# Running the first MoE1 chunk in two halves of 256 tokens, with a new order of attention units and other PSUM banks

## The chip, the cores and the metric

The kernel runs on one core of one Trainium2 chip. The metric is the device time of one execution in microseconds (us), lower is better. Times of one kernel spread by up to 2.4 us here, so comparisons below are against runs of the kernel before on the same chip, in the same rounds, unless the text says otherwise. Engine names as in the profile: PE is TensorE, PEld its weight loads, ACT is ScalarE, DVE is VectorE, POOL is GpSimd, SP is SyncE.

## The reference

Sliding-window attention with ALiBi (8 batches, 8 heads, 576 tokens, head size 64, window 128) feeds a two-layer gated MLP over all 4608 tokens:

```python
scores = scale * q @ k.T + slopes[h] * -(pos_q - pos_k)   # only 0 <= pos_q - pos_k < 128
attn   = softmax(scores) @ v
x      = attn, as [4608 tokens, 512]
h      = x @ w_in            # 512 -> 2048, "MoE1" in the kernel
g      = h * cos(h)
out    = g @ w_out           # 2048 -> 512, "MoE2"
```

## The kernel before

The kernel records operations with their data dependencies and a priority. A list scheduler of its own then fixes one static order per engine, and semaphores are put in where engines depend on each other. PE executes its list strictly in that order.

Tokens go through the MLP in nine chunks of 512. Chunk `c` is worked on while attention for batch `c + 1` runs, so most attention work hides beside matmuls. Chunk 0 has no such cover: attention for batch 0 has to be done first. It has nine units: `(pr, G)` is head pair `pr` with queries `256*G` to `256*G + 255`, and `"t"` is the tail, queries 512 to 575, of all heads.

```python
def units(b):
    if b == 0:
        return [(pr, G) for p0 in range(2) for G in range(2) for pr in (p0, p0 + 2)] + [
            ("t", None)]
    return [("t", None)] + [(pr, G) for pr in range(NPAIR) for G in range(2)]
```

Each unit is: scores (PE), exponential (ACT), mask product (DVE), product with v (PE), normalization (DVE), transposition back into `xT` (PE, then a copy by ACT or DVE). MoE1 needs all four pairs, as they are its contraction dimension:

```python
def moe1(c, fc, bank):
    ...
    for kc in range(NPAIR):
        op("pe", lambda e, kc=kc: e.matmul(
            ps[:, bank, :], w_in[:, kc, 128 * fc:128 * fc + 128], xT[:, kc, r0:r0 + CH],
            start=(kc == 0), stop=(kc == NPAIR - 1)), ...)      # 512 columns
    op("act", ... ACTF.Sin, bias=halfpi ...)                    # cos, 128x512
    op("dve", ... gT[gi][:, fc, :] = ps * cos ...)              # 128x512
...
if c == 0:
    for fc in range(NFC):                                       # 16 groups
        moe1(c, fc, (OB + UB)[fc % 4])
    for pl in range(2):
        qk_transposes("q", pl, SB[0:2])
        qk_transposes("k", pl, SB[2:4])
```

There are eight PSUM banks: `SB` (4 to 7) for scores, `UB` (2, 3) for products with v and the transpositions back, `OB` (0, 1) for MoE2 results. In chunk 0 a MoE1 group uses one of banks 0 to 3, and two of these belong to attention until its tail is done. One more rule of the scheduler matters: exponential and cosine are functions of different tables on ACT, and all exponentials of a batch come before the first cosine of the chunk.

The softmax here doesn't subtract the row's maximum and nothing guards it: scores larger than these inputs give would overflow.

Of the kernel before, what the change touches and what calls it, by code (L numbers as in the profile page):

```python
# [6 lines left out]
ALU = mybir.AluOpType  # L7
ACTF = mybir.ActivationFunctionType
# [3 lines left out]
B, H, S, D = 8, 8, 576, 64  # L12
NPAIR = H // 2
# [4 lines left out]
NFC = DFF // 128  # L18
CH = 512
# [15 lines left out]
class Plan:  # L35
# [12 lines left out]
    def op(self, eng, fn, r=(), w=(), dma=None, occ=100, lat=None, pri=5, mode=0, table=None):  # L48
        o = Op()
        o.seq = len(self.all)  # L50
        o.eng = (eng,) if isinstance(eng, str) else tuple(eng)
        o.fn, o.r, o.w, o.dma = fn, tuple(r), tuple(w), dma
        o.occ, o.lat, o.pri, o.mode, o.table = occ, occ if lat is None else lat, pri, mode, table
        preds = {}
        for k in o.r:
            if k in self.writer:
                preds[self.writer[k]] = DATA
        for k in o.w:
            if k in self.writer:
                preds[self.writer[k]] = DATA  # L60
            for d in self.readers.get(k, ()):
                preds.setdefault(d, WAR)
        if dma is not None and dma in self.lastdma:
            preds[self.lastdma[dma]] = DATA
        if eng in ("pool", "sp"):
            if eng in self.lastseq:
                preds.setdefault(self.lastseq[eng], ORDER)
            self.lastseq[eng] = o
        if dma is not None:
            self.lastdma[dma] = o  # L70
        o.preds, o.succs, o.npred = preds, [], len(preds)
        for d in preds:
            d.succs.append(o)
        for k in o.r:
            self.readers.setdefault(k, []).append(o)
        for k in o.w:
            self.writer[k], self.readers[k] = o, []
        self.all.append(o)
        return o
# [160 lines left out]
def bass_alibi_sliding__then__act_gcu_kernel(  # L240
# [8 lines left out]
    with ExitStack() as ctx:  # L249
# [4 lines left out]
        op = R.op  # L254

        w_in = sb("w_inb", [128, 4, DFF])
        w_out = sb("w_outb", [128, NFC, DMODEL])
        XR = 3 * CH
        xT = sb("xT", [128, NPAIR, XR])
        gT = [sb(f"gT{i}", [128, NFC, CH]) for i in range(2)]  # L260
# [11 lines left out]
        NCOS = 3  # L272
        cosb = [sb(f"cos{i}", [128, 512], F32) for i in range(NCOS)]
# [90 lines left out]
        def qk_transposes(which, pl, banks):  # L364
            jj = ((0, 5), (5, 9))

            def dst(n):
                return ps[:, banks[n], :].bitcast(BF16)[:, 0:128 * (jj[n][1] - jj[n][0])]

            def f(e):  # L370
                ins = None
                for n, (j0, j1) in enumerate(jj):
                    for j in range(j0, j1):
                        for x in range(2):
                            ins = e.transpose(  # L375
                                dst(n)[64 * x:64 * x + 64, 128 * (j - j0):128 * (j - j0) + 128],
                                qB[which][:, 2 * pl + x, 64 * j:64 * j + 64], ident[:, :])
                return ins
            op("pe", f, r=[("qB", which, pl), "ident"], w=[("B", x) for x in banks],
               occ=500, lat=670, mode=2, pri=3)  # L380
            for n, (j0, j1) in enumerate(jj):
                o = tr[which][:, :].rearrange("p (g l t) -> p g l t", g=2, l=2)[
                    :, :, pl, 0:576].rearrange("p g (s j) -> p g s j", j=9)[:, :, :, j0:j1]
                i = dst(n).rearrange("p (j g s) -> p g s j", j=j1 - j0, g=2)
                op(("act", "dve"),
                   {"act": lambda e, o=o, i=i: e.activation(o, i, ACTF.Copy),  # L386
                    "dve": lambda e, o=o, i=i: e.tensor_copy(o, i)},
                   w=[("B", banks[n]), ("tr", which, pl, j0)],
                   occ={"act": (730, 620)[n], "dve": (750, 620)[n]},
                   lat={"act": (840, 735)[n], "dve": (815, 690)[n]}, pri=4)  # L390
# [6 lines left out]

        def units(b):
            if b == 0:
                return [(pr, G) for p0 in range(2) for G in range(2) for pr in (p0, p0 + 2)] + [  # L400
                    ("t", None)]
            return [("t", None)] + [(pr, G) for pr in range(NPAIR) for G in range(2)]

        def scores(b, us):
# [140 lines left out]
        def xkeys(pr, t0, n):  # L545
            return [("xT", pr, (t // 64) % (XR // 64)) for t in range(t0, t0 + n, 64)]
# [42 lines left out]
        ccount = [0]  # L589

        def moe1(c, fc, bank):
            ci = ccount[0] % NCOS
            ccount[0] += 1
            gi = c % 2
            r0 = (CH * c) % XR
# [3 lines that stand above are left out]
                    start=(kc == 0), stop=(kc == NPAIR - 1)),  # L599
                   r=xkeys(kc, CH * c, CH) + [("wi", fc // 4)], w=[("B", bank)],  # L600
                   occ=216, lat=379, pri=5)
            op("act", lambda e: e.activation(cosb[ci][:, :], ps[:, bank, :], ACTF.Sin,  # L602
                                             bias=halfpi[:, 0:1]),
               r=["halfpi"], w=[("B", bank), ("cos", ci)], occ=586, lat=687, table=2 * c + 1,
               pri=3)
            op("dve", lambda e: e.tensor_tensor(gT[gi][:, fc, :], ps[:, bank, :], cosb[ci][:, :],  # L606
                                                ALU.mult),
               r=[("cos", ci)], w=[("B", bank), ("g", gi, fc)], occ=606, lat=692, pri=3)

        def moe2(c):  # L610
            gi = c % 2
            for t in range(4):
                tg = 4 * c + t
                bank = OB[tg % 2]
                oi = tg % NOB
                for fc in range(NFC):
                    op("pe", lambda e, t=t, fc=fc, bank=bank: e.matmul(  # L617
                        ps[:, bank, :], gT[gi][:, fc, 128 * t:128 * t + 128], w_out[:, fc, :],
                        start=(fc == 0), stop=(fc == NFC - 1)),
                       r=[("g", gi, fc), ("wo", fc // 4)], w=[("B", bank)], occ=216, lat=379,  # L620
                       pri=6)
                op(("act", "dve"),
                   {"act": lambda e, bank=bank, oi=oi: e.activation(  # L623
                       ob[oi][:, :], ps[:, bank, :], ACTF.Copy),
                    "dve": lambda e, bank=bank, oi=oi: e.tensor_copy(ob[oi][:, :], ps[:, bank, :])},
                   w=[("B", bank), ("ob", oi)], occ={"act": 490, "dve": 606},
                   lat={"act": 591, "dve": 691}, pri=6)
                row = CH * c + 128 * t
                op("sp", [lambda e, oi=oi, row=row: e.dma_start(out[row:row + 128, :],
                                                                ob[oi][:, :])],  # L630
                   r=[("ob", oi)], dma=f"st{oi}", occ=60, lat=600)
# [34 lines left out]
        for c in range(NCH):  # L666
            if c < B - 1:
                if c == 0:
                    for fc in range(NFC):
                        moe1(c, fc, (OB + UB)[fc % 4])  # L670
                    for pl in range(2):
                        qk_transposes("q", pl, SB[0:2])
                        qk_transposes("k", pl, SB[2:4])
                else:
                    qk_transposes("q", 0, SB[0:2])
                    qk_transposes("k", 0, SB[2:4])
                    for fc in range(NFC):
                        if fc == 8:
                            qk_transposes("q", 1, SB[0:2])
                        if fc == 12:  # L680
                            qk_transposes("k", 1, SB[0:2])
                        moe1(c, fc, (UB + SB + UB + SB[2:] + UB + SB[2:] + UB)[fc])
                if c + 2 < B:
                    for pl in range(2):
                        load_qk("q", q, c + 2, pl)
                        load_qk("k", k, c + 2, pl)
                    load_v(c + 2, (3, 4, 0, 1, 2))
                attention(c + 1)
            else:
                for fc in range(NFC):  # L690
                    moe1(c, fc, (UB + SB)[(16 * c + fc) % 6])
            moe2(c)
# [29 lines left out]
```

## Time and profile before

| | before |
|---|---|
| median time | 353.36 us (353.24 to 354.44, 3 runs) |
| span of the profiled run | 351.4 us |
| PE busy | 334.0 us, 95% |
| PE idle from 80 to 340 us | 0.50 us |
| tail exponential of batch 0 ends | 25.46 us |
| first cosine starts | 31.63 us |
| last MoE1 matmul of chunk 0 | 47.4 us |

The page of the profile: the span, the busy times with their shares, then the busy tenths of PE in 40 equal slices and the granted clock in tenths.

```profile
span 351.4 us, 7156 instructions
...
PE 334.0 (95%) x2912; PEld 167.2 (48%) x2912; DVE 206.2 (59%) x451; ACT 236.2 (67%) x347; POOL 79.8 (23%) x121
...
PE   2768999999999999999999999999999999999996
```

PE is full from the fifth slice on. What can be won lies in the first four slices, about 35 us. The table of stretches of PE alone gives them in finer steps; the columns are the stretch in us, its length, PE's busy time with its instruction count, the granted clock, the DMA share and GB/s.

```profile
20.00:22.00 2.00, 2.00 (x18) 1.00 1.24 206
22.00:24.00 2.00, 1.54 (x36) 1.00 1.24 206
24.00:26.00 2.00, 0.98 (x24) 1.00 1.23 206
26.00:28.00 2.00, 1.37 (x13) 0.60 1.22 205
28.00:30.00 2.00, 1.90 (x6) 0.55 1.21 203
30.00:32.00 2.00, 1.53 (x36) 1.00 1.21 203
32.00:60.00 28.00, 27.43 (x272) 1.00 1.42 175
```

PE idles about 2.7 us between 22 and 32 us, and its clock falls to about half at 26 to 30 us. From 32 to 60 us only 0.57 us are idle. The clock column shows 1.00 wherever the trace holds no clock record yet; here the first record is a rise to full at 22.98 us, and PE ran at half speed before it (experiments 1 and 6 come back to this). The timeline of ACT (start, duration, engine and line, operation, out from in, count, and in brackets the idle time before with what ended it):

```profile
24.43 1.03 ACT L447 ACTIVATE ptail<-ps 128x1024 bf16<-128x1024 f32 x1
26.92 0.72 ACT L583 ACTIVATE xT<-ps 128x256 bf16<-128x256 bf16 x2 [1.45 <-PE ps L569]
29.94 0.38 ACT L583 ACTIVATE xT<-ps 128x256 bf16<-128x256 bf16 x1 [2.30 <-PE ps L569]
30.34 1.28 ACT L602 ACT_TABLE_LOAD   x1
31.63 1.27 ACT L602 ACTIVATE cos<-ps,halfpi 128x512 f32<-128x512 f32 x2
```

ACT ends its last exponential at 25.46 us, then waits 1.45 and 2.30 us for PE, because the copies into `xT` stand ahead of the table load in its order. The timeline of PE:

```profile
27.79 1.90 PE L597 MATMUL ps<-xT,w_inb 128*128 128x512 bf16 x4
...
38.13 9.45 PE L597 MATMUL ps<-xT,w_inb 128*128 128x512 bf16 x43
47.42 4.05 PE L617 MATMUL ps<-w_outb,gT 128*128 128x512 bf16 x18
51.89 0.19 PE L491 MATMUL ps<-vp,ptail 128*128 128x65 bf16 x1 [0.42 <-DVE ptail L463]
```

The first line is MoE1 at half clock: 1.90 us for four matmuls, whose modelled ends overlap; in the chain of waits (from the last instruction back, at each step to what released it) they take 1.71 us, 0.43 us each. The 43 matmuls of the second line take 9.40 us in that chain, 0.219 us each. The last line shows the largest later gap before 60 us, 0.42 us.

### The profile page before, as it was taken

What the parts mean: (1) busy time and instruction counts of PE and PEld (TensorE: products, weight loads), DVE (VectorE), ACT (ScalarE), POOL (GpSimd) and SP (SyncE); (2) the same over time, 40 slices, a digit from 0 to 9 for tenths busy, and PEclk for the clock granted to TensorE, in tenths of its full rate; (3) what the DMA queues carried; (4) which work ended last, traced back from release to release, by engine and by line L of the source; (5) the groups of instructions that cost most, each with busy time, mean ns of one, the idle gap of its engine ahead of it and who ended that gap; (6) DMA issues with size and microseconds to landing.
All of it is one profiled execution on the core that took longest, in us unless ns stands there. A gap on an engine that the chain in (4) does not pass through costs nothing.

```text
span 351.4 us, 7156 instructions
## 1 busy us (share of the span) xinstructions
PE 334.0 (95%) x2912; PEld 167.2 (48%) x2912; DVE 206.2 (59%) x451; ACT 236.2 (67%) x347; POOL 79.8 (23%) x121
## 2 busy tenths in 40 slices
PE   2768999999999999999999999999999999999996
PEld 2434445544644554455445644464445444444442
DVE  2486768677858777793576645692768254065000
ACT  3875888987878788877667876786777564155121
POOL 8993700252207021602150207000000000000000
PEclk9998999999999999999999999999999999999999
DMA  6999999449148833915291329400011000100212
GB/s 91 163 207 205 194 186 107 69 68 98 36 93 89 103 48 49 131 47 97 48 137 43 73 55 118 81 32 29 2 41 52 0 32 17 74 32 30 90 62 90
DMA packets 56160, 28.25 MB, mean 80 GB/s; under 512 B 39232, under 2 KB 51520, under 8 KB 56128
## 3 DMA queue, kind: packets, MB, share of 16 engines
q0 software_dynamic: 50944, 18.36, 47.0%
q1 hardware_dynamic: 5184, 9.44, 7.2%
q8 instruction: 23, 0.38, 0.4%
q14 instruction: 9, 0.07, 0.1%
HBM read 36.70 MB, written 9.44 MB: 131 GB/s over the span
## 4 chain that ended last, share of the span: by engine, by line
PE 90%; ACT 3%; DVE 2%; POOL 2%; DMA 1%; issue 1%; POOLq 0%; ACTq 0%
PE ps L597 37%; PE ps L617 33%; PE ps L375 5%; PE ps L425 5%; PE ps L505 3%; PE ps L569 2%; PE ps L508 2%; DMA krows<-in_k_dram 1%; ACT ptail L447 1%; DVE ptail L463 1%; PE ps L491 1%; ACT L447 1%; POOL qrows L298 1%; PE ps L415 1%; PE ps L493 1%
## 5 line engine op out<-in xcount | busy, mean ns | idle before, releaser
L617 PE MATMUL ps<-w_outb,gT 128*128 128x512 bf16 x576 | 138.7, 379 | 0.0
L597 PE MATMUL ps<-xT,w_inb 128*128 128x512 bf16 x576 | 137.7, 382 | 0.0
L606 DVE TENSOR_TENSOR gT<-ps,cos 128x512 bf16<-128x512 f32 x144 | 92.1, 686 | 70.5 <-PE ps L617 55.9
L602 ACT ACTIVATE cos<-ps,halfpi 128x512 f32<-128x512 f32 x144 | 93.2, 689 | 29.0 <-PE ps L617 13.4
L597 PEld LDWEIGHTS ps<-xT,w_inb 128*128 128x128 bf16 x576 | 52.2, 98 | 62.8 <-DVE gT L606 7.3
L617 PEld LDWEIGHTS ps<-w_outb,gT 128*128 128x128 bf16 x576 | 53.9, 98 | 58.7 <-issue 2.2
L455 ACT ACTIVATE p<-ps 128x768 bf16<-128x768 f32 (+1 forms) x64 | 56.2, 916 | 16.4 <-PE ps L425 15.5
L298 POOL DMA_DIRECT2D qrows<-in_q_dram x32 | 19.8, 634 | 129.3 <-PE ps L375 61.6
L623 ACT ACTIVATE ob<-ps 128x512 f32<-128x512 f32 x31 | 18.5, 597 | 44.7 <-PE ps L617 44.7
L470 DVE TENSOR_TENSOR p<-p,emask 128x768 bf16<-128x768 bf16 (+1 forms) x64 | 39.3, 617 | 2.0 <-ACT p L455 1.9
L307 POOL DMA_DIRECT2D vp<-in_v_dram x40 | 34.1, 906 | 0.0
L539 DVE TENSOR_TENSOR xnat<-ps,rec 128x256 bf16<-128x256 f32 x64 | 26.4, 418 | 0.5
L505 PE MATMUL ps<-vp,p 128*128 128x65 bf16 x256 | 22.9, 199 | 0.8 <-DVE xT L584 0.4
L425 PE MATMUL ps<-qt,kt 64*128 64x128 bf16 (+1 forms) x320 | 20.6, 253 | 1.5 <-ACT kt L386 1.0
L505 PEld LDWEIGHTS ps<-vp,p 128*128 128x128 bf16 x256 | 17.0, 100 | 9.8 <-DVE xT L584 3.4
L298 POOL DMA_DIRECT2D krows<-in_k_dram x32 | 19.6, 636 | 8.5 <-PE ps L597 7.5
L569 PE MATMUL ps<-ident,xnat 128*128 128x128 bf16 x128 | 18.5, 229 | 2.7 <-DVE xnat L539 2.7
L583 ACT ACTIVATE xT<-ps 128x256 bf16<-128x256 bf16 (+3 forms) x36 | 12.6, 353 | 12.0 <-PE ps L569 11.8
L508 PE MATMUL ps<-vp,p 128*128 128x65 bf16 x192 | 20.6, 197 | 0.0
L386 ACT ACTIVATE kt<-ps 128x640 bf16<-128x640 bf16 (+1 forms) x21 | 15.8, 777 | 4.3 <-PE ps L375 4.3
L375 PE MATMUL ps<-ident,qrows 128*64 128x128 bf16 x288 | 12.1, 233 | 6.0 <-POOL ident L339 6.0
L537 DVE RECIPROCAL rec<-ps 128x4 f32<-128x4 f32 x64 | 11.2, 178 | 8.7 <-PE ps L508 7.3
(44 smaller groups left out, 200.2 us busy)
## 6 DMA issues: line engine op xcount, KB each, us to landing
out_dram<-ob SPq DMA_DIRECT2D x36, 256.0 KB, 2.0
qrows<-in_q_dram POOLq DMA_DIRECT2D x32, 144.0 KB, 3.4
krows<-in_k_dram POOLq DMA_DIRECT2D x32, 144.0 KB, 4.1
vp<-in_v_dram POOLq DMA_DIRECT2D x32, 128.0 KB, 4.5
w_inb<-in_moe_w_in_dram POOLq DMA_DIRECT2D x4, 512.0 KB, 10.0
w_outb<-in_moe_w_out_dram POOLq DMA_DIRECT2D x4, 512.0 KB, 18.5
vp<-in_v_dram POOLq DMA_DIRECT2D x8, 64.0 KB, 4.2
```

The lines of the kernel that those rows point to most:

```text
L298: fns.append(lambda e, g=g: e.dma_start(qB[which][64 * g:64 * g + 64, 2 * pl:2 * pl + 2, :], src[b, 4 * g + 2 * pl:4 * g + 2 * pl + 2, :, ...
L307: op("pool", [lambda e, t=t, rows=rows: e.dma_start(vp[b % 2][0:rows, t, :, 0:64], v[b, :, 128 * t:128 * t + rows, :].rearrange("h p d -> ...
L375: ins = e.transpose(dst(n)[64 * x:64 * x + 64, 128 * (j - j0):128 * (j - j0) + 128], qB[which][:, 2 * pl + x, 64 * j:64 * j + 64], ident[: ...
L425: ins = e.matmul(ps[:, banks[x], c0:c1], keys_ap(x, pr, kc), query_ap(x, pr, qb, 128 * nb), start=True, stop=True)
L455: op("act", lambda e: e.activation(P[i][:, :, lo:512], src_[:, :, lo:512], ACTF.Exp, scale=0.125), w=held + [("P", i)], occ=920 if u[1] el ...
L470: op("dve", lambda e: e.tensor_tensor(P[i][:, :, lo:512], P[i][:, :, lo:512], EM[:, 2 * pr:2 * pr + 2, lo:512], ALU.mult), r=[("P", i), (" ...
L505: ins = e.matmul(o, P[i][:, x, d0:d0 + 128], V[:, kc, h, 0:65], start=True, stop=not two)
L508: ins = e.matmul(o, P[i][:, x, p0:p0 + 128], V[:, kc - 1, h, 0:65], start=False, stop=True)
L597: op("pe", lambda e, kc=kc: e.matmul(ps[:, bank, :], w_in[:, kc, 128 * fc:128 * fc + 128], xT[:, kc, r0:r0 + CH], start=(kc == 0), stop=(k ...
L602: op("act", lambda e: e.activation(cosb[ci][:, :], ps[:, bank, :], ACTF.Sin, bias=halfpi[:, 0:1]), r=["halfpi"], w=[("B", bank), ("cos", c ...
L606: op("dve", lambda e: e.tensor_tensor(gT[gi][:, fc, :], ps[:, bank, :], cosb[ci][:, :], ALU.mult), r=[("cos", ci)], w=[("B", bank), ("g", ...
L617: op("pe", lambda e, t=t, fc=fc, bank=bank: e.matmul(ps[:, bank, :], gT[gi][:, fc, 128 * t:128 * t + 128], w_out[:, fc, :], start=(fc == 0 ...
```

## The change

Its intent: work for PE should be there earlier. The units of batch 0 are reordered so that the first queries of all pairs come first; MoE1 of chunk 0 runs in two halves of 256 tokens, so that half 0 needs four units instead of eight; and its groups use six banks, the score banks included, once the scores are done. A group now holds two values of `fc` for 256 tokens, so the cosines and products keep shape and count.

```diff
-                return [(pr, G) for p0 in range(2) for G in range(2) for pr in (p0, p0 + 2)] + [
-                    ("t", None)]
+                return [(pr, G) for G in range(2) for pr in (0, 2, 1, 3)] + [("t", None)]
@@ new, beside moe1, used for chunk 0 only (cut)
+        def moe1_half(c, hf, f2, bank):
+            ...
+            t0 = CH * c + 256 * hf
+            for i in range(2):
+                fc = 2 * f2 + i
+                for kc in range(NPAIR):
+                    op("pe", lambda e, i=i, fc=fc, kc=kc: e.matmul(
+                        ps[:, bank, 256 * i:256 * i + 256], w_in[:, kc, 128 * fc:128 * fc + 128],
+                        xT[:, kc, r0:r0 + 256], start=(kc == 0), stop=(kc == NPAIR - 1)),
+                       r=xkeys(kc, t0, 256) + [("wi", fc // 4)], w=[("B", bank)], ...)
+            op("act", ... cosine of 128x512 ...)
+            op("dve", ... product into gT[gi][:, 2 * f2:2 * f2 + 2, 256 * hf:256 * hf + 256] ...)
@@ moe2 waits for its half only
-                       r=[("g", gi, fc), ("wo", fc // 4)], ...
+                       r=[("g", gi, fc, t // 2), ("wo", fc // 4)], ...
@@ chunk 0
-                    for fc in range(NFC):
-                        moe1(c, fc, (OB + UB)[fc % 4])
+                    for i in range(NFC):
+                        moe1_half(c, i // 8, i % 8, (OB + SB)[i] if i < 6 else (OB + SB)[i % 4])
                     for pl in range(2):
-                        qk_transposes("q", pl, SB[0:2])
+                        qk_transposes("q", pl, SB[2:4])
                         qk_transposes("k", pl, SB[2:4])
```

More of the change, by code (lines that the diff above doesn't have):

```diff
@@ L607, in moe1 @@
                                                 ALU.mult),
-               r=[("cos", ci)], w=[("B", bank), ("g", gi, fc)], occ=606, lat=692, pri=3)
+               r=[("cos", ci)], w=[("B", bank), ("g", gi, fc, 0), ("g", gi, fc, 1)], occ=606, lat=692, pri=3)
+        def moe1_half(c, hf, f2, bank):
+            ci = ccount[0] % NCOS
+            ccount[0] += 1
+            gi = c % 2
+            t0 = CH * c + 256 * hf
+            r0 = t0 % XR
+            for i in range(2):
[4 more added lines that the diff above has]
+                        xT[:, kc, r0:r0 + 256], start=(kc == 0), stop=(kc == NPAIR - 1)),
+                       r=xkeys(kc, t0, 256) + [("wi", fc // 4)], w=[("B", bank)],
+                       occ=108, lat=271, pri=5)
+            op("act", lambda e: e.activation(cosb[ci][:, :], ps[:, bank, :], ACTF.Sin,
+                                             bias=halfpi[:, 0:1]),
+               r=["halfpi"], w=[("B", bank), ("cos", ci)], occ=586, lat=687, table=2 * c + 1,
+               pri=3)
+            op("dve", lambda e: e.tensor_tensor(
+                gT[gi][:, 2 * f2:2 * f2 + 2, 256 * hf:256 * hf + 256],
+                ps[:, bank, :].rearrange("p (i t) -> p i t", i=2),
+                cosb[ci][:, :].rearrange("p (i t) -> p i t", i=2), ALU.mult),
+               r=[("cos", ci)], w=[("B", bank)] + [("g", gi, 2 * f2 + i, hf) for i in range(2)],
+               occ=606, lat=692, pri=3)
         def moe2(c):
@@ L619, in moe2 @@
                         start=(fc == 0), stop=(fc == NFC - 1)),
-                       r=[("g", gi, fc), ("wo", fc // 4)], w=[("B", bank)], occ=216, lat=379,
+                       r=[("g", gi, fc, t // 2), ("wo", fc // 4)], w=[("B", bank)], occ=216, lat=379,
                        pri=6)
```

## The prediction

> **What bounds the kernel now.** TensorE. The page's busy table gives PE 334.0 us of a 351.4 us span (95%), and the busy table by stretches shows PE idle for only 0.5 us of the 240 us between 80 and 320 us. So the time is "when PE becomes dense" plus a fixed amount of PE work. The lost time is at the start: the timeline shows PE gaps until about 30.5 us (PE busy 2.68 of 5 us at 15-20, 3.92 at 20-25, 3.86 at 25-30), and the granted clock falls to 0.60 and 0.55 at 26-30 us, where a 512-column matmul takes 0.43 us instead of 0.216. One later gap, 0.42 us at 51.5 us, waits for the mask of the next batch's tail.
>
> Why PE starves: MoE1 of chunk 0 needs all 512 tokens, that is all eight attention units; the last xT copies end at 30.3 us. Only 8 of its 64 matmuls are done by 32.3 us, its first cosine runs at 31.6 us (the table load waits behind those copies, 30.3-31.6), and its last matmul ends at 47.4 us.
>
> **What the change does.** First-query units of all four head pairs go first, so half 0 of MoE1 can start when four units are done. 64 matmuls of 512 columns become 128 of 256: the same columns, so about 0.108 us each (half of 0.216, an estimate); 64 more weight loads (98 ns each) stay under the matmuls, as the page shows PEld at 48%. The Trainium skill, "TensorE: Matmul & The Clock Gate", section on throughput, gives N/2.4 + 2.5 ns for an isolated gap, so at most 0.2 us extra in all. Cosines (0.69 us) and products (0.69 us) keep their count, 16. Six PSUM banks can hold half 0, so PE may run six groups before a cosine ends. Two q transposes move banks; negligible.
>
> **Size.** ACT still has to do the mask exponentials, eight unit exponentials and the tail; I expect its tail exponential to end at 25-25.5 us as before (25.46). But the table load now follows at once, so cosines start near 26.8 instead of 31.6 us. W_in quarters landed at 19.9, 22.1, 24.7 and 27.4 us (issue plus landing time), just soon enough. PE then has dense work from about 26.4 us: 112 half matmuls 12.1 us, q/k transposes 4 x 0.62, remaining attention 1.2 us, about 0.5 us stalls on ACT/DVE (16 cosines plus five q/k copies fill ACT for about 14 us in the same stretch). MoE1 ends at about 42.6 us. Before, it ended at 47.4, 0.5 us of that being next-batch scores that now come later: gain about 4.3 us. The 0.42 us gap should vanish, as 23 instead of 18 MoE2 matmuls cover that chain. W_out (last quarter 43.4 us) and the next v (44.2-48.0 us) should land just before use. All saved time is PE-critical, nothing later gives it back.
>
> **Prediction:** 348.9 us, 80% range 346.7 to 351.2. Faster by over 2% 0.08, within 2% 0.91, slower by over 2% 0.01.
>
> **What would show the steps right:** MoE1 matmuls of 128x256 spaced about 0.108 us once the clock is up; first cosine at 26-28 us; granted clock near 1.0 in 25-30 us; last MoE1 matmul at 41.5-44 us; no PE gap before the next tail's product; PE busy total about unchanged or slightly lower while the span falls by 4-5 us; from 60 us on the same stream, shifted.
>
> **What would make it wrong:** PE, in order, stuck behind a MoE1 matmul waiting for w_in while scores wait behind it, delaying the exponentials; the clock staying at half until 30 us (costs up to 2 us); ACT and DVE, nearly full at 26-42 us, pacing the MoE1 groups; DMA (about 205 GB/s up to 40 us) bringing w_out or v too late; 256-column matmuls slower than half.

(The section of the Trainium skill meant there, in "TensorE: Matmul & The Clock Gate", is "Back-to-back issue gap". The 0.2 us is an estimate from that page's 2.5 ns: 64 more matmuls make 0.16 us.)

## The result

| | before | changed |
|---|---|---|
| median time, same rounds | 353.81 us (4 runs) | 349.19 us (348.81 to 349.53, 4 runs) |
| ratio, first comparison | | 0.9869 (95%: 0.9845 to 0.9892) |
| ratio, repeated in other rounds (below) | | 0.9864 (0.9845 to 0.9883) |
| span of the profiled run | 351.4 us | 346.8 us |
| PE busy | 334.0 us | 331.8 us |
| tail exponential of batch 0 ends | 25.46 us | 25.56 us |
| first cosine starts | 31.63 us | 26.87 us |
| last MoE1 matmul of chunk 0 | 47.4 us | 42.6 us |

A ratio is the mean time of one kernel's fast runs over that of the other's of the same rounds, so it is not quite the ratio of the medians quoted. At 1.3% the change is within the 2% that count as the same, but clear of noise.

The page of the changed kernel:

```profile
span 346.8 us, 7278 instructions
...
PE 331.8 (96%) x2976; PEld 172.4 (50%) x2976; DVE 203.9 (59%) x452; ACT 235.7 (68%) x346; POOL 79.6 (23%) x121
...
PE   2689999999999999999999999999999999999996
```

PE is full one slice earlier. Its table of stretches:

```profile
20.00:22.00 2.00, 2.00 (x19) 1.00 1.25 207
22.00:24.00 2.00, 1.72 (x31) 1.00 1.24 206
24.00:26.00 2.00, 2.00 (x43) 1.00 1.23 205
26.00:28.00 2.00, 2.00 (x27) 1.00 1.22 204
28.00:30.00 2.00, 1.85 (x29) 1.00 1.23 210
30.00:32.00 2.00, 2.00 (x25) 1.00 1.19 199
32.00:60.00 28.00, 28.00 (x372) 1.00 1.41 176
```

The hole is gone, and the clock no longer falls. From 32 to 60 us PE has no idle time at all, so neither w_out nor v came late. The timeline of ACT:

```profile
24.53 1.03 ACT L446 ACTIVATE ptail<-ps 128x1024 bf16<-128x1024 f32 x1
25.58 1.28 ACT L624 ACT_TABLE_LOAD   x1
26.87 1.27 ACT L624 ACTIVATE cos<-ps,halfpi 128x512 f32<-128x512 f32 x2
```

The table load follows the last exponential at once. The timeline of PE:

```profile
30.05 2.67 PE L619 MATMUL ps<-xT,w_inb 128*128 128x256 bf16 x23
...
40.16 2.58 PE L619 MATMUL ps<-xT,w_inb 128*128 128x256 bf16 x22
42.57 1.89 PE L642 MATMUL ps<-w_outb,gT 128*128 128x512 bf16 x8
```

The last line is the first of MoE2: MoE1 ends there. The MoE1 matmuls of 256 columns cost just half of those of 512: 2.51 us for 23 in the chain of waits is 0.109 us each. The Trainium skill ("TensorE: Matmul & The Clock Gate", section "Back-to-back issue gap") gives N/2.4 + 2.5 ns for an isolated gap at full clock, an estimate of 109.2 ns for 256 columns; the trace agrees.

The chain of waits of the changed kernel (start, duration, what), from the stretch before PE becomes dense:

```profile
20.49 1.21 PE ps L619 x5
21.70 0.98 PE ps L424 x12
...
22.71 1.94 ACT p L454 x2
24.65 0.92 ACT ptail L446
...
25.58 1.28 ACT L624
...
26.87 0.70 ACT cos L624
...
27.59 0.69 DVE gT L628
28.29 0.34 DVE xnat L538
...
28.67 0.28 PE ps L568 x2
28.96 0.77 PE ps L619 x7
```

So in the changed kernel the chain goes through the last exponentials, the table load, the first cosine and product, and reaches PE at 28.67 us. From there to 60 us the chain runs through PE alone. The chain also passes through five early MoE1 matmuls (L619 x5) that stand before the last scores.

**Where the 4.6 us of span came from.** An estimate from the two traces, for what follows the end of the tail exponential (25.5 us in both). By then PE had done 13 half matmuls instead of 2 whole ones, worth about 1.0 us (13 x 0.108 less 2 x 0.216). PE idle after that point was 2.5 us before (0.27 us to 26 us, then 0.63, 0.10, 0.47, 0.57 in the stretches above and 0.50 us from 80 to 340 us); it is now 0.65 us (0.15 at 28 to 30, 0.17 at 60 to 80 and 0.33 us from 80 to 340). That is 1.9 us. The four MoE1 matmuls at half clock lost 0.85 us (1.71 less 4 x 0.216), and the products and transpositions beside them some 0.3 us. Together about 4.0 of 4.6 us. The last two terms, about 1.2 us, are what the clock cost directly.

### The profile page after: what moved, and what is told of

The parts are those of the page before. It is cut to its first block, busy times and chain, and to the rows that moved or that the text cites. A ratio compares the mean times of both kernels' runs of the same rounds, so it can differ in the third digit from the quotient of the medians.

```text
span 346.8 us, 7278 instructions
## 1 busy us (share of the span) xinstructions
PE 331.8 (96%) x2976; PEld 172.4 (50%) x2976; DVE 203.9 (59%) x452; ACT 235.7 (68%) x346; POOL 79.6 (23%) x121
## 4 chain that ended last, share of the span: by engine, by line
PE 90%; ACT 4%; POOL 2%; DMA 1%; DVE 1%; issue 1%; POOLq 0%; ACTq 0%
PE ps L642 34%; PE ps L596 33%; PE ps L375 5%; PE ps L424 5%; PE ps L619 3%; PE ps L504 3%; PE ps L568 2%; PE ps L507 2%; DMA krows<-in_k_dram 1%; ACT ptail L446 1%; ACT L446 1%; PE ps L490 1%; POOL qrows L298 1%; DVE ptail L462 1%; ACT p L454 1%
## 5 line engine op out<-in xcount | busy, mean ns | idle before, releaser
L605 DVE TENSOR_TENSOR gT<-ps,cos 128x512 bf16<-128x512 f32 x128 | 81.5, 686 | 70.0 <-PE ps L642 53.7
L596 PE MATMUL ps<-xT,w_inb 128*128 128x512 bf16 x512 | 121.0, 380 | 0.0
L601 ACT ACTIVATE cos<-ps,halfpi 128x512 f32<-128x512 f32 x128 | 82.4, 688 | 25.9 <-PE ps L642 13.4
L596 PEld LDWEIGHTS ps<-xT,w_inb 128*128 128x128 bf16 x512 | 46.1, 98 | 56.1 <-DVE gT L605 7.1
L582 ACT ACTIVATE xT<-ps 128x256 bf16<-128x256 bf16 (+3 forms) x34 | 11.9, 353 | 8.2 <-PE ps L568 8.1
L386 ACT ACTIVATE kt<-ps 128x640 bf16<-128x640 bf16 (+1 forms) x20 | 15.0, 780 | 3.5 <-PE ps L375 3.2
L386 ACT ACTIVATE qt<-ps 128x512 bf16<-128x512 bf16 (+1 forms) x21 | 15.3, 756 | 2.7 <-PE ps L375 2.3
```

The source lines that it names most:

```text
L386: {"act": lambda e, o=o, i=i: e.activation(o, i, ACTF.Copy), "dve": lambda e, o=o, i=i: e.tensor_copy(o, i)},
L596: op("pe", lambda e, kc=kc: e.matmul(ps[:, bank, :], w_in[:, kc, 128 * fc:128 * fc + 128], xT[:, kc, r0:r0 + CH], start=(kc == 0), stop=(k ...
L601: op("act", lambda e: e.activation(cosb[ci][:, :], ps[:, bank, :], ACTF.Sin, bias=halfpi[:, 0:1]), r=["halfpi"], w=[("B", bank), ("cos", c ...
L605: op("dve", lambda e: e.tensor_tensor(gT[gi][:, fc, :], ps[:, bank, :], cosb[ci][:, :], ALU.mult), r=[("cos", ci)], w=[("B", bank), ("g", ...
```

## The experiments

Theory A: the gain comes from MoE1 work that fills the PE hole of 20 to 30 us, for which the halves are needed. Rivals: B, the order of units alone (earlier cosine); C, the six banks alone; D, the early start without the banks; G, the clock, which no longer falls. The edits are against the changed kernel unless said otherwise. All kernels gave correct results. Numbers are collected in a table after the last one.

### 1. Order alone

```diff
 the kernel before
-                return [(pr, G) for p0 in range(2) for G in range(2) for pr in (p0, p0 + 2)] + [
-                    ("t", None)]
+                return [(pr, G) for G in range(2) for pr in (0, 2, 1, 3)] + [("t", None)]
```

> The kernel before with only the order of units of batch 0 changed (first queries of all four pairs first, MoE1 still 512 tokens wide in banks 0 to 3). Theory A (the gain comes from MoE1 work that can fill the TensorE hole of 20 to 30 us, which needs the half chunks): a 512-token MoE1 still waits for all eight units, so the hole stays; expect -0.5 us against before (between -1.5 and +0.5). Rival B (the order alone, through the earlier end of the exponentials, table load and first cosine): -3.5 to -4.6 us.

Measured: ratio 0.9948 (0.9920 to 0.9975), 352.62 against 354.31 us, about -1.8 us. That is more than A expected and about half of the least that B expected. The trace shows the hole still there (PE busy 1.39 us at 24 to 26 and 1.48 us at 26 to 28):

```profile
24.00:26.00 2.00, 1.39 (x21) 1.00 1.23 205
26.00:28.00 2.00, 1.48 (x14) 1.00 1.21 203
28.00:30.00 2.00, 2.00 (x19) 1.00 1.21 203
```

The clock column's 1.00 must not be believed here. The trace's first clock record, a rise to full, is at 31.02 us, and the three matmuls of this line of PE's timeline start 0.427 us apart, which is half speed:

```profile
27.94 1.49 PE L596 MATMUL ps<-xT,w_inb 128*128 128x512 bf16 x3
```

The first cosine started at 30.78 us. B is out as the main cause. Of the -1.8 us the one trace shows 0.4 us (span 351.0 us). That trace was at half speed for longer than the trace of the kernel before, which may hide a part; the rest is open.

### 2. Old order, with halves and six banks

```diff
-                return [(pr, G) for G in range(2) for pr in (0, 2, 1, 3)] + [("t", None)]
+                return [(pr, G) for p0 in range(2) for G in range(2) for pr in (p0, p0 + 2)] + [
+                    ("t", None)]
```

> The changed kernel with the old order of units. Theory A: half 0 is now complete after six units instead of four, with the same six banks; MoE1 starts later, most of the hole is still filled from about 26 us on; expect -3 us against before (-2 to -4). Rival B (order alone is the cause): about 0.

Measured: 0.9870 (0.9850 to 0.9891), -4.4 us by the medians, more than the -2 to -4 that A expected and as good as the changed kernel in other rounds. This was a surprise: it made the new order look worthless. It was run again beside the changed kernel (experiment 5).

### 3. New order and six banks, chunk 0 whole

```diff
-                        moe1_half(c, i // 8, i % 8, (OB + SB)[i] if i < 6 else (OB + SB)[i % 4])
+                        moe1(c, i, (OB + SB)[i] if i < 6 else (OB + SB)[i % 4])
```

> The changed kernel (new order, six banks, q transposes moved) with MoE1 of chunk 0 again 512 tokens wide. Theory A: only the matmuls of the pairs that are done can run early, no group can be finished before all eight units are; expect -2 us against before (-1 to -3), first cosine about 29 us. Rival C (the six banks, not the halves, are what lets TensorE run ahead): -4 to -4.6 us.

Measured: 0.9913 (0.9892 to 0.9935), -3.0 us; first cosine at 30.27 us. Two thirds of the gain without halves, at the upper edge of what A expected. Not all of it, so C is not the whole cause either.

### 4. New order and halves, old banks

```diff
-                        moe1_half(c, i // 8, i % 8, (OB + SB)[i] if i < 6 else (OB + SB)[i % 4])
+                        moe1_half(c, i // 8, i % 8, (OB + UB)[i % 4])
                     for pl in range(2):
-                        qk_transposes("q", pl, SB[2:4])
+                        qk_transposes("q", pl, SB[0:2])
```

> The changed kernel (new order, halves) with MoE1 of chunk 0 in the four old banks, two of which attention uses until the tail is done. Theory A with banks as a necessary part: only two groups (16 of 64 half matmuls) can be done before the tail, so most of the hole stays; expect -2 us against before (-1 to -3). Rival D (the halves and the early start alone are enough, banks do not matter): -4 to -4.6 us.

Measured: 0.9923 (0.9904 to 0.9941), -2.7 us. The first cosine comes at 26.89 us, as early as in the changed kernel, and yet PE is busy for only 0.87 us of the stretch 26 to 28 us. An early start that has no bank to go on with leaves PE waiting. D is out.

### 5. The changed kernel again, and experiment 2 beside it

> The changed kernel once more, on the same chip as the next three. Expect ratio 0.987 (0.985 to 0.989), and a spread of about 1 us between its runs.

> The changed kernel with the old order of units again, now beside the changed kernel on one chip, because the first run left open how much the order is worth. Theory A1: the order has a use of its own, as TensorE had only 29 instead of 42 half matmuls behind it when the tail product came (30.0 us in both) and started MoE2 at 44.5 instead of 42.6 us in the two traces; expect +0.7 us against the changed kernel (+0.3 to +2). Rival B2: the order is worth nothing (within 0.3 us).

Measured: the changed kernel 0.9864 (348.77 us), the old order 0.9892 (0.9875 to 0.9910; 349.68 us), both against 353.33 us. The medians differ by 0.9 us and no run of one reached the other (348.26 to 348.93 against 349.15 to 350.10). So the order has a use of its own, about 0.9 us, once the halves are there.

### 6. Dummy matmuls that keep the clock up, in the changed kernel

Between 2 and 40 matmuls of 124 columns, whose result nobody reads, are put before each of ten PE operations that have to wait, between 1 and 20 us. They write PSUM banks that no other engine uses at that time; free columns of a bank in use would not do, for the reason that the Trainium skill gives ("PSUM — Partial Sum Buffer", section "PSUM bank collisions raise a hardware error"): two engines may not be in one bank and quadrant at once, even at different columns. No run here shows such a collision.

```diff
+        R.fill({0: (40, 7, None), 1: (20, 7, None), 2: (20, 7, None), 4: (14, 0, None),
+                5: (18, 7, (0, (2, 0))), 7: (10, 0, None), 9: (2, 0, None), 11: (4, 0, None),
+                12: (12, 0, None), 14: (6, 0, None)}, ...)   # PE op: (count, bank, wait for exp)
         R.emit(final=[f"st{i}" for i in range(NOB)])
```

> The changed kernel with dummy matmuls of 124 columns (result thrown away) put into the TensorE waits between 1 and 20 us, so that the clock is at full speed from the start. Until 23 us the changed kernel's matmuls run at half speed (43 to 44 to 52 ns between 65-column products, 0.22 us per 256-column matmul), about 2.7 us of dense work from 20.3 to 23 us. Theory A (what is left of the loss is the cold clock while dense, and the early chain): -1.5 us against the changed kernel (-0.7 to -2.5). Rival F (the early stretch is bound by DMA arrivals, ScalarE and VectorE, so the clock does not matter): within 0.5 us.

Measured: 0.9825 (0.9801 to 0.9849), 347.09 us, 1.7 us below the changed kernel of the same rounds. Theory A's number held, rival F fell. The five MoE1 matmuls before the last scores now took 0.72 instead of 1.42 us. The clock column had shown 1.00 for this stretch in the changed kernel, while its 65-column products stood 52 to 57 ns apart, against 30 ns later on. The trace's first clock record is a rise to full at 23.01 us; before the first record the column does not tell the clock, and the spacing does. With the dummies the first rise is at 5.83 us.

### 7. MoE1 held behind the last scores

```diff
-            op("pe", f, r=keys, w=held, occ=occ, lat=occ + 165, mode=1, pri=2)
+            op("pe", f, r=keys, w=held + ([("lastsc",)] if b == 0 and us[0][0] == (1, 1) else []),
+               occ=occ, lat=occ + 165, mode=1, pri=2)
@@ moe1_half
-                       r=xkeys(kc, t0, 256) + [("wi", fc // 4)], w=[("B", bank)],
+                       r=xkeys(kc, t0, 256) + [("wi", fc // 4), ("lastsc",)], w=[("B", bank)],
```

> The changed kernel with all MoE1 matmuls of chunk 0 held behind the last scores of batch 0, so that the five of them that ran at 20.3 to 21.6 us no longer stand before those scores (the chain of waits passes through them, 1.21 us, then scores, exponentials, table load, cosine). Theory A (TensorE is dense from 20 us either way, so an earlier exponential buys little): -0.2 us against the changed kernel (-0.6 to +0.4), with the tail exponential ending 0.6 to 1 us earlier. Rival E (the chain through the exponentials and the cosine sets the time): -0.8 us or more.

Measured: 0.9850 (0.9827 to 0.9873), 348.36 us; the changed kernel had 0.9864. The difference is within the noise. The test did not do what it was to do: the tail exponential ended at 25.91 us, no earlier, as the six MoE1 matmuls then stood before the tail's scores instead. So it tells nothing about E.

### 8. Dummy matmuls in the kernel before

```diff
 the kernel before
+        R.fill({21: (6, 7, X), 23: (14, 7, X), 25: (6, 7, X), 30: (3, 7, X), 31: (9, 7, X)}, ...)
+        # X = (0, (3, 1)): after that unit's exponential
```

(Thirty-eight dummies as listed; the expectation says 44, a miscount.)

> The kernel before with 44 dummy matmuls of 124 columns in its TensorE waits between 24.4 and 30.5 us, so that the clock does not fall to half at 26 to 30 us. Theory A (the gain of the change is filled waits first, and only in part the clock): about 1.1 to 1.3 us of matmul time at half speed goes away (four 512-column matmuls at 0.43 instead of 0.216 us, eight products and two transposes at 52 instead of 33 ns and 110 instead of 57 ns), so -1.2 us against before (-0.5 to -1.8). Rival G (the change gains mostly by keeping the clock up): -3.5 us or more.

Measured: 0.9989 (0.9965 to 1.0013), 352.91 against 353.35 us. In its trace the clock fell at 18.18 us and rose again only at 28.42 us:

```profile
16.00:20.00 4.00, 2.15 (x30) 0.77 1.23 202
20.00:22.00 2.00, 2.00 (x20) 0.50 1.24 207
...
26.00:28.00 2.00, 2.00 (x24) 0.50 1.21 204
28.00:30.00 2.00, 2.00 (x28) 0.90 1.21 203
```

The dummies then cost twice their time and pushed work back (14 of them took 1.64 us). So it does not measure what a fast clock at 26 to 30 us is worth, and it does not test G. Two things in the other traces speak against G as the main cause. By count, half speed cost the kernel before about 1.2 of the 4.6 us (above). And the traces of experiments 4 and 9 were at full clock from 23.80 and 23.34 us on, yet what follows their tail exponential is 2.5 and 1.6 us longer than in the changed kernel (table below). The clock's exact share stays open.

### 9. Banks alone

```diff
 the kernel before
-                        moe1(c, fc, (OB + UB)[fc % 4])
+                        moe1(c, i, (OB + SB)[i] if i < 6 else (OB + SB)[i % 4])
                     for pl in range(2):
-                        qk_transposes("q", pl, SB[0:2])
+                        qk_transposes("q", pl, SB[2:4])
```

> The kernel before with only the PSUM banks of chunk 0 changed (six banks for MoE1 that attention has left, q transposes moved); old order, 512 tokens wide. Order plus banks gave -3.1 us and order alone -1.8 us. Theory A (each part lets more MoE1 work into the hole; parts overlap): -1.5 us (-0.5 to -2.5). Rival C (banks carry most of it): -3 us or more.

Measured: 0.9941 (0.9917 to 0.9965), 351.26 against 353.35 us, -2.1 us, within what A expected. The six banks are worth something with no other part of the change.

### 10. Experiments 6 and 7 together

The fill of experiment 6 (13 instead of 18 before operation 5, 8 instead of 6 before operation 14, which is now the last scores) on the kernel of experiment 7.

> The two variants that were faster than the changed kernel together: dummy matmuls in the early waits and MoE1 behind the last scores of batch 0. Against before: 0.9825 for the dummies alone, 0.985 for the late MoE1 alone, 0.9864 for the changed kernel in the same rounds. If the two add up: -0.3 us more than the dummies alone, ratio 0.981 to 0.982, which would make it the fastest here. If late MoE1 helps only because it shortens a stretch at half clock: no better than the dummies alone (0.9825).

Measured: 0.9822 (0.9797 to 0.9848), 347.04 us. Not measurably better than the dummies alone; the interval also holds the 0.981 to 0.982 expected if the two add up, so this is not decided. By the ratios both are about 0.4% faster than the changed kernel and 1.8%, some 6.3 us, faster than the kernel before. Experiment 6 shows the first in the same rounds; these two versions beat both kernels.

### 11. The second q and k loads before the mask constants

```diff
             if pl == 0:
-                constants()
+                make_ident()       # the identity alone
+        constants()                # the mask constants, without it
```

> The changed kernel with the second q and k loads of batch 0 issued before the mask constants on POOL (identity first), to ask what bounds the stretch before 20 us. In four traces the second k landed at 12.0 to 13.8 us and TensorE and ScalarE waited for it. Theory H (its landing sets the early stretch): it lands about 1 us earlier, -0.7 us against the changed kernel (-0.3 to -1.3). Rival I (ScalarE sets it; its mask exponentials now start near 8 instead of 5.2 us, about 1.2 us of its work moves into the full stretch): +0.5 us or more.

Measured: 0.9924 (0.9899 to 0.9949), 350.63 us. By the ratios that is 0.6%, about 2 us, above the changed kernel (0.9864 to 0.9869, in other rounds). The second k landed at 11.5 instead of 12.5 us, and it did not help: the first mask exponential came at 9.80 instead of 5.21 us, ACT's first unit exponential started at 12.08 us (10.99 us in the repeated changed kernel) and the tail exponential ended at 27.49 us. H fell. Rival I's number held, but that ScalarE sets the early stretch is not shown: the chain of waits between 10 and 28 us passes through only one mask exponential (0.53 us), ACT waited 3.3 us for PE's scores there (1.8 us in the repeated changed kernel), and PE was at half speed until 26.46 instead of 24.21 us.

### What the traces have in common

Numbers of all kernels, and the span less the end of batch 0's tail exponential, both from the trace. The last column says from when PE's clock was at full speed, by the clock records in the trace file:

| kernel | ratio to before | tail exp. ends | span | difference | clock full from |
|---|---|---|---|---|---|
| before | 1 | 25.46 | 351.4 | 325.9 | 22.98 to 26.39, again from 29.80 |
| dummies in before | 0.9989 | 25.31 | 351.6 | 326.3 | 14.76 to 18.18, again from 28.42 |
| order | 0.9948 | 25.24 | 351.0 | 325.8 | 31.02 |
| order, halves | 0.9923 | 25.57 | 349.3 | 323.7 | 23.80 |
| order, banks | 0.9913 | 25.51 | 349.1 | 323.6 | 27.07 |
| banks | 0.9941 | 25.81 | 348.6 | 322.8 | 23.34 |
| halves, banks | 0.9870, 0.9892 | 25.90, 25.32 | 348.4, 347.5 | 322.5, 322.2 | 26.97, about 25.3 (by spacing) |
| order, halves, banks (the change) | 0.9869, 0.9864 | 25.56, 25.79 | 346.8, 347.0 | 321.2, 321.2 | 23.01, 24.21 |
| the change, MoE1 late | 0.9850 | 25.91 | 347.1 | 321.2 | 24.97 |
| the change, dummies | 0.9825 | 24.87 | 346.0 | 321.1 | 5.83 |
| the change, dummies, MoE1 late | 0.9822 | 23.30 | 344.5 | 321.2 | 5.95 |
| the change, k loads first | 0.9924 | 27.49 | 348.7 | 321.2 | 26.46 |

The last six traces agree within 0.1 us, although the tail exponential ends anywhere from 23.30 to 27.49 us. The two extremes, first dummies with late MoE1, then k loads first, in the timeline of ACT, each with the line that heads the answer:

```profile
core 0 of [0], span 344.5 us
...
22.27 1.03 ACT L465 ACTIVATE ptail<-ps 128x1024 bf16<-128x1024 f32 x1
```

```profile
core 0 of [0], span 348.7 us
...
26.47 1.02 ACT L449 ACTIVATE ptail<-ps 128x1024 bf16<-128x1024 f32 x1
```

4.20 us later here, 4.2 us longer there. In the changed structure what follows the tail exponential is a fixed amount of dense PE work, so whatever shortens or lengthens the early stretch moves the end one to one. It is not shown that the end waits for the exponential itself. The chain of waits passes through it in four of the six traces. In those of experiments 7 and 11 it passes by it, in experiment 7 through PE alone, because the tail's scores (L414) stand in PE's fixed order, and the exponential and PE's later work move together:

```profile
22.58 1.28 PE ps L620 x6
...
24.30 0.54 PE ps L414 x13
```

Against the kernel before, the difference column gives order 0.1, banks 3.1, order and banks 2.3, halves with order but without banks 2.2, halves and banks 3.4 to 3.7, all three 4.7 us. This is free of the scatter of the first 25 us, but not of the clock. In the last six traces the clock was full before the tail exponential ended. Behind it, half speed added about 2.2 us of matmul time with the order alone (a count: 6 matmuls of 512 columns at 0.21, 24 products at 0.025, 6 transpositions at 0.05 us more), about 1.3 us in the kernel before by the same count, and about 0.5 us with order and banks and in the first trace of halves and banks; some of it fell into waits. So the order alone is probably worth more than 0.1 us, and a part of the other values may be the clock's. The parts overlap, and none is the whole; the halves alone were not run. By the trace the banks alone give most; by the rounds they do not (2.1 us, against 3.0 for order and banks and 2.7 for order and halves on another chip).

It is one trace per kernel, and the timed ratios don't follow it everywhere: banks alone is -3.1 us by the trace and -2.1 us by the rounds, order alone -0.1 and -1.8 us. What varies between runs of one kernel is not settled. Two things do vary in the traces: the second k landed between 12.00 and 13.87 us in those of experiments 5 and 6, and the clock rose at different times (last column). The runs of the kernel before point to the clock too. Of 27 in the later rounds, the 12 whose mean clock reads 0.994 or 0.995, as in its trace, have spans of 350.4 to 351.7 us, and the 7 that read 1.00, as the trace of the order alone does, 352.0 to 352.9 us. Without their traces this stays a guess.

## Why the prediction was right

The prediction was 348.9 us (346.7 to 351.2); the time was 349.19 us, and 348.77 us when repeated.

- **Bound: PE, time lost at the start.** Right. PE idle from 22 to 32 us went from 2.7 to 0.4 us, and the later stream only moved.
- **256-column matmuls cost half.** Right: 0.109 us.
- **Table load at once, first cosine near 26.8 us.** Right: 26.87 us, after a tail exponential that ended at 25.56 us as before.
- **Dense from about 26.4 us, MoE1 ends at 42.6 us.** Right in its end, 42.57 us. Small errors offset each other. By 26.4 us PE had done 20 half matmuls, so 108 were left and not 112 (11.8 us against 12.1); the q/k transposes took 2.5 us as expected (2.48) and the rest of attention 1.1 us (1.2); time between matmuls beyond their usual spacing came to about 0.7 us, more than the 0.5 us allowed for stalls.
- **The 0.42 us gap goes, w_out and v arrive in time.** Right: no PE idle time at all from 32 to 60 us.
- **Reason given for the gain.** It held for the change as a whole, but the prediction gave the weight to half 0 becoming ready after four units, and named the banks in passing. The runs put it otherwise: the six banks alone win about 2 (rounds) or 3 us (trace), the order adds about 0.9 us on top of halves and banks and won 1.8 us alone in its rounds, and with the new order in both, halves without the banks (2.7 us) win no more than banks without the halves (3.0 us).
- **The risk of PE stuck behind early MoE1 matmuls.** It happened: five of them at half clock, 20.28 to 21.63 us, stand before the last scores in the chain, and ACT waits 1.79 us there. The stretch still ended on time.
- **Clock.** The prediction expected it near full at 25 to 30 us, and it was. It did not see that the matmuls before 23 us run at half speed under a clock column of 1.00; filling the waits there won another 1.7 us.

## What to carry to other kernels

Where PE starves at the start of a pipeline, ask both what makes work ready earlier and where its results may go: without a free PSUM bank the earliest work stops after a group or two. Once the hole is filled, the time follows the early stretch before it one to one, so look there next, PE's own speed in it included. And read PE's clock from the spacing of equal matmuls, not from a clock column that has no record yet; a start at half speed can be cut by dummy matmuls in waits (experiment 6; in experiment 8 they did not help), if they write banks that no other engine is using.

## What the Trainium skill lacked or had wrong

- "TensorE: Matmul & The Clock Gate", section "Back-to-back issue gap": its sustained figure of about 131 ns per 512-column matmul was not reached. The 43 in a row of chunk 0 took 219 ns each, close to the formula of that section (N/2.4 + 2.5, 215.8 ns), which it says over-counts.
- The same page, section "The HAM clock gate (the "warmup" mystery)", says that the window runs freely and that half rate is the default, and this agrees: the first lasting rise to full clock came at 23.01 and 24.21 us in two traces of the changed kernel and at 31.02 us with the order alone, and until then matmuls stood at half-speed spacing. It gives no busy share that counts as busy, and the runs give no clean one. In the trace of experiment 8 the records are multiples of 3.41 us apart; PE was busy 2.65 and 2.72 us of the two stretches of 3.41 us from 18.18 us and stayed at half, then 3.41 us and rose. In experiment 3 it rose after 2.80 us, in experiment 2 it did not after 3.10 us.
- The same page, section "Seeing it yourself", warns that clock records can be wrong. No run here shows that: in the changed kernel the first record, the rise at 23.01 us, is where the spacing of 65-column products falls from 52 to 57 ns towards 30 ns. What misled was the column of the profile, which reads 1.00 before the first record; in experiment 1 that was up to 31.02 us.
- "ScalarE: Activation LUTs", section "What ACT_TABLE_LOAD costs", adds a drain of about 1380 ns to each load of 1283 ns. The load took 1.28 us here too; of the drain nothing is seen. The exponential ended at 25.56, the load began at 25.58 and ended at 26.86, and the cosine began at 26.87 us.
